# Spectral filter and gated feed-forward on one core: a later hold for the filter loads, and other PSUM banks and filler for the first batch's blocks

## The chip, the cores and the metric

One core of one Trainium2 chip. The metric is the device time of one execution in microseconds (us). Two things are used: the ratio of runs made on the same chip in the same rounds, and stage boundaries read from traces.

## The reference

```python
X = np.fft.rfft(x, axis=1)                      # x: (8, 3008, 256) float32
y = np.fft.irfft(X * (filt_r + 1j * filt_i)[None], n=3008, axis=1)
y = y.reshape(8 * 3008, 256)
out = (np.maximum(y @ w_gate, 0) * (y @ w_val)) @ w_out     # 256 -> 1536 -> 256
```

The kernel computes the transforms as matmuls in two steps (3008 = 94 x 32). A forward step over 94 (`psA`) goes out to device memory (`Abuf`) and comes back in another order (`at`). A forward step over 32 (`psX`), the products with the two filters (`tt`, `uu`) and an inverse step (`psD`) follow, then a second trip through memory (`Dbuf`, `dC`) and the last inverse step (`psY`). `psV`, `psG` and `psO` are the feed-forward part, which fills the rest of the time. Batches 1 to 7 are transformed in the shadow of the feed-forward blocks. Only batch 0 stands before the first of them, and only batch 0 is touched by this change.

## The kernel before

The parts that matter. Code of one engine runs in the order in which it is written here.

```python
def hold_gpsimd(tile_):                      # GpSimd waits until tile_ is there
    scr = sb.tile([128, 8], FP32, tag="scr", bufs=2)
    nc.gpsimd.tensor_copy(scr[:tile_.shape[0]], tile_)

def warm(n, cols=512):                       # filler: keeps TensorE's clock up
    psJ = ps.tile([128, 512], FP32, tag=fft_tag(True), name="psJ")
    for i in range(n):
        nc.tensor.matmul(psJ[:, :cols], junk[:, 0:128], junk[:, :cols], start=True, stop=True)
# ... the prologue:
load_x(0, nc.sync, ...)                      # x of batch 0 to XF[0], XF[1], 5 pieces
load_own_filters()
hold_gpsimd(XF[0][:, 2 * q - 8:2 * q])       # a quarter of x is there
for _ in filters:                            # the 7 other filter loads, on GpSimd's queue
    pass
warm(11)
for i, f in enumerate(items_a(0)):           # psA -> asb -> Abuf
    f()
    if i == 12:
        load_at(0, 0)
        load_at(0, 1)
for c in range(2, 4):
    load_at(0, c)
for half in range(2):
    for a in range(2):
        place_filter(0, a, half, nc.vector.tensor_copy)     # Ftr, waits for its loads
for i in range(3):
    make_back_t(i)                           # TensorE psI, VectorE copies it to I2t
warm(6)
place_filter(1, 0, 0, nc.vector.tensor_copy)
for i in range(3):
    make_back_u(i)                           # TensorE reads I2t
# ... place_own, the rest of Fti
for i in range(15):
    warm(2)                                  # 30 fillers until at is there
# ...
def first_b(amid):
    cuts = (0, 2, 4, 5, 6)
    for i in range(6):
        fwd(0, i)                            # psX, two banks by rotation over three pairs
        if i > 1:
            inv(0, i - 2, cuts=cuts)         # psD, the same rotation; ScalarE copies to dsb
        for e in range(2):
            product(0, i, e, 0)
            product(0, i, e, 1, pool=(i, e) in POOL_U)
        amid(i)                              # i < 2: warm(4, 256); else psA items of batch 1
    inv(0, 4, cuts=cuts)
    amid(6)
    inv(0, 5, cuts=cuts)
```

## Time and profile before

| | before |
|---|---|
| median of 4 runs (range) | 895.88 us (895.24 to 896.71) |
| span of the profiled run | 895.1 us |
| first forward block (`psX`) starts | 36.08 us |
| last `dsb` of first B ends | 53.32 us |
| first `psV` starts | 61.87 us |

Read it backwards. The feed-forward part is bound by TensorE and moves as a whole with its start, at 61.87. What counts is when the first `psX` starts, how long first B takes from there (53.32 - 36.08 = 17.24 us), and the last trip through memory.

### The profile page before, as it was taken

To read this page: it belongs to the slowest core of one execution; us is meant where nothing else is said; L and a number is where in the kernel's file an instruction comes from. 1 tells how busy PE (TensorE), PEld (TensorE's weight loads), DVE (VectorE), ACT (ScalarE), POOL (GpSimd) and SP (SyncE) were. 2 spreads that over 40 slices of the span, in tenths; PEclk is the share of its full clock that TensorE was granted. 3 is DMA by queue.
4 is the path that set the end of the run, shared out by engine and by line. 5 is a ranking of instruction groups with operands and counts; after the bars stand their busy time and mean duration, and the time that the engine had idled before them with its cause. 6 is when DMAs were issued, how large, how long until landed. Compare 5 with 4: busy or idle time off the path is not lost.

```text
span 895.1 us, 19152 instructions
## 1 busy us (share of the span) xinstructions
PE 878.4 (98%) x7206; PEld 507.2 (57%) x7206; DVE 569.2 (64%) x873; ACT 498.8 (56%) x891; POOL 364.4 (41%) x361
## 2 busy tenths in 40 slices
PE   7999999999999999999999999999999999999997
PEld 2335555556556665566655566555655566566665
DVE  2637766577665776666766676657776577655553
ACT  3475555555555556556555556555655555555552
POOL 4351698038661486416672167802867000000001
PEclk9999999999999999999999999999999999999999
DMA  8998448434466336463375334762445512331111
GB/s 229 281 242 170 131 132 179 110 102 121 122 152 135 117 95 146 129 139 94 97 175 139 92 99 108 179 139 78 118 138 148 121 31 80 81 74 36 37 34 51
DMA packets 114099, 109.18 MB, mean 122 GB/s; under 512 B 20359, under 2 KB 98599, under 8 KB 113366
## 3 DMA queue, kind: packets, MB, share of 16 engines
q1 hardware_dynamic: 90294, 80.10, 34.7%
q0 software_dynamic: 22992, 26.41, 12.3%
q8 instruction: 57, 0.93, 0.5%
q10 hardware_dynamic: 720, 1.45, 0.5%
q14 instruction: 36, 0.29, 0.1%
HBM read 61.93 MB, written 49.81 MB: 125 GB/s over the span
## 4 chain that ended last, share of the span: by engine, by line
PE 94%; DMA 2%; ACT 1%; POOL 1%; SPq 1%; DVE 1%; issue 1%; ACTq 0%; POOLq 0%
PE psV L467 28%; PE psG L467 27%; PE psO L486 27%; PE psF L323 3%; PE psD L394 2%; PE psY L451 2%; PE psX L364 2%; PE psA L276 1%; DMA XF<-in_x_dram 1%; PE psJ L520 1%; SPq L176 1%; DVE prod L472 0%; ACT dsb L401 0%; DMA dC<-Dbuf 0%; POOL out_dram L509 0%
## 5 line engine op out<-in xcount | busy, mean ns | idle before, releaser
L472 DVE SCALAR_TENSOR_TENSOR prod<-psG,vsb 128x512 bf16<-128x512 f32 x564 | 389.0, 690 | 263.4 <-ACT vsb L470 257.5
L470 ACT CAST vsb<-psV 128x512 bf16<-128x512 f32 x564 | 331.9, 589 | 263.2 <-PE psV L467 162.8
L467 PE MATMUL psV<-yT,WvT 128*128 128x512 bf16 x1128 | 336.6, 380 | 0.8 <-ACT asb L330 0.5
L486 PE MATMUL psO<-WoT,prod 128*128 128x256 bf16 x2256 | 336.5, 273 | 0.0
L467 PE MATMUL psG<-yT,WgT 128*128 128x512 bf16 x1128 | 335.5, 379 | 0.9 <-ACT dsb L401 0.3
L486 PEld LDWEIGHTS <-prod 128*128 128x128 bf16 x2256 | 220.3, 98 | 143.7
L467 PEld LDWEIGHTS <-WgT 128*128 128x128 bf16 x1128 | 109.9, 97 | 136.4 <-issue 3.4
L467 PEld LDWEIGHTS <-WvT 128*128 128x128 bf16 x1128 | 98.5, 98 | 41.8 <-issue 30.5
L258 POOL CAST scr<-prod 128x8 f32<-128x8 bf16 x24 | 4.5, 189 | 257.7 <-DVE prod L472 257.7
L509 POOL DMA_DIRECT2D out_dram<-osb x5 | 2.6, 536 | 195.9 <-ACT osb L499 195.9
L499 ACT COPY osb<-psO 128x512 f32<-128x512 f32 x92 | 53.9, 586 | 28.0 <-PE psO L486 26.6
L380 DVE TENSOR_TENSOR tt<-psX,Ftr 128x512 bf16<-128x512 f32 x96 | 65.1, 682 | 6.8 <-PE psX L364 6.8
L309 POOL TENSOR_TENSOR fold<-XP 128x1024 f32<-128x1024 f32 x24 | 56.6, 2357 | 20.8 <-PE psF L323 19.4
L380 DVE TENSOR_TENSOR uu<-psX,Fti 128x512 bf16<-128x512 f32 x89 | 60.5, 680 | 0.0
L401 ACT CAST dsb<-psD 128x512 bf16<-128x512 f32 x96 | 51.5, 589 | 12.5 <-PE psD L394 12.4
L296 POOL DMA_DIRECT2D XP<-in_x_dram x96 | 56.7, 596 | 3.2 <-PE psG L467 1.6
L310 POOL TENSOR_TENSOR XP<-XP 128x1024 f32<-128x1024 f32 x24 | 56.4, 2349 | 1.9
L330 ACT CAST asb<-psF 128x512 bf16<-128x512 f32 x48 | 25.8, 589 | 30.5 <-PE psF L323 30.5
L330 DVE CAST asb<-psF 128x512 bf16<-128x512 f32 x48 | 30.9, 686 | 18.6 <-PE psF L323 18.6
L456 ACT CAST yT<-psY 128x512 bf16<-128x512 f32 x47 | 27.5, 586 | 22.9 <-PE psY L451 22.6
L458 DVE CAST yT<-psY 128x512 bf16<-128x512 f32 x47 | 32.0, 681 | 9.7 <-PE psY L451 9.7
L451 PE MATMUL psY<-M,dC 96*128 96x94 bf16 (+18 forms) x604 | 37.5, 199 | 0.5 <-DMA dC<-Dbuf 0.4
(70 smaller groups left out, 493.3 us busy)
## 6 DMA issues: line engine op xcount, KB each, us to landing
at<-Abuf SPq DMA_DIRECT2D x32, 384.0 KB
dC<-Dbuf SPq DMA_DIRECT2D x64, 192.0 KB
XP<-in_x_dram POOLq DMA_DIRECT2D x48, 256.0 KB, 5.9
Dbuf<-dsb SPq DMA_DIRECT2D x23, 512.0 KB
XP<-in_x_dram POOLq DMA_DIRECT2D x96, 96.0 KB, 2.6
Abuf<-asb SPq DMA_DIRECT2D x96, 96.0 KB
out_dram<-osb SPq DMA_DIRECT2D x69, 94.0 KB
XF<-in_x_dram SPq DMA_DIRECT2D x15, 256.0 KB
```

Source lines behind the costliest of these rows:

```text
L296: nc.gpsimd.dma_start(xp[r:r + 24, 0:4:2, :], _ap(x, (b * N1 * N2 + o) * D, [[N2 * D, 24], [47 * N2 * D, 2], [1, 512]]))
L309: tt(t, xp[:, 0:2], xp[:, 2:4], op=ALU.add)
L310: tt(xp[:, 2:4], xp[:, 0:2], xp[:, 2:4], op=ALU.subtract)
L330: copy(asf[:, :, q, :], banks[q])
L380: nc.vector.tensor_tensor(p, psX, filt, op=ALU.mult)
L401: nc.scalar.copy(dsb[:, a, o:o + 2, :], psD[a])
L451: nc.tensor.matmul(psY[:, o:o + w], dCs[b, n2 // 8][:, n2 % 8, h * 128:(h + 1) * 128], M1[:, n1:n1 + w], start=True, stop=True)
L467: nc.tensor.matmul(pt[:, :W], w[:, h, ft * 128:(ft + 1) * 128], yt[:, h, :], start=(h == 0), stop=(h == 1))
L470: nc.scalar.copy(vsb, psV[:, :W])
L472: nc.vector.scalar_tensor_tensor(prod, in0=psG[:, :W], scalar=0.0, in1=vsb, op0=ALU.max, op1=ALU.mult)
L486: nc.tensor.matmul(psO[:, t % 2], prods[ft][:, t * 128:(t + 1) * 128], WoT[:, ft, :], start=(ft == 0), stop=(ft == NFT - 1))
L499: copy(osb[:, t0 % 2:t % 2 + 1], psO[:, t0 % 2:t % 2 + 1])
```

## The change

Its intent: x gets the DMA engines to itself for longer, so that the chain from x to `psX` ends sooner. Filler goes to where TensorE would otherwise idle in front of the first three forward blocks. Inverse blocks get banks of their own.

```diff
-    def fwd(b, i):
+    def fwd(b, i, junks=0):
         for e in range(2):
-            psXs[b, i, e] = ps.tile([128, 2, D], FP32, tag=fft_tag(), name="psX")
+            tag = "fft" if b or not e else "psv"
+            psXs[b, i, e] = ps.tile([128, 2, D], FP32, tag=tag, name="psX")
+            for _ in range(junks):
+                nc.tensor.matmul(psXs[b, i, e], junk[:, 0:128], junk, start=True, stop=True)
 ...
-        cuts = (0, 2, 4, 5, 6)
+        cuts, tags = (0, 2, 4, 5, 6), ("psg", "psg")
         for i in range(6):
-            fwd(0, i)
+            fwd(0, i, 2 if i < 3 else 0)
             if i > 1:
-                inv(0, i - 2, cuts=cuts)
+                inv(0, i - 2, tags, cuts)
 ...
-    hold_gpsimd(XF[0][:, 2 * q - 8:2 * q])
+    hold_gpsimd(XF[0][:, 4 * q - 8:4 * q])
 ...
     def amid(i):
-        if i < 2:
-            warm(4, 256)
-        else:
+        if i > 1:
             for _ in range((1, 1, 2, 1, 1)[i - 2]):
                 next(early)()
```

(The other lines of the diff move the tile `junk` up and pass `tags` on.)

## The prediction

> **What bounds the kernel now.** I read four views in this order: the page, the chain of work that ended last, the timeline engine by engine from 0 to 66 us, and the windows of one microsecond for the granted clock. First the page.
>
> ```profile
> PE 878.4 (98%) x7206; PEld 507.2 (57%) x7206; DVE 569.2 (64%) x873; ACT 498.8 (56%) x891; POOL 364.4 (41%) x361
> PE 94%; DMA 2%; ACT 1%; POOL 1%; SPq 1%; DVE 1%; issue 1%; ACTq 0%; POOLq 0%
> ```
>
> TensorE is busy for 98% of the span, and is 94% of the chain. The change touches nothing after batch 0, so it cannot shorten that part; it can only start it sooner. The first gate matmul of the main loop (psV) starts at 61.87 us of 895.1. So all that is at stake lies in the first 62 us, 7% of the span. A 2% verdict would need 18 us out of those 62.
>
> In that stretch "busy" misleads, because filler (psJ) counts as busy. The chain there shows it, from the last of x to the first forward block:
>
> ```profile
> 13.49 8.74 DMA XF<-in_x_dram
> 22.48 3.65 PE psA L276 x8
> 26.13 0.67 PE psI L192 x45
> 26.80 1.40 PE psJ L520 x6
> 28.20 0.74 PE psI L202 x3
> 28.94 6.49 PE psJ L520 x30
> 35.43 0.65 issue
> 36.08 0.46 PE psX L364 x8
> ```
>
> The columns are start, length and what. After the last piece of x come 3.65 us of forward DFT, then 9.30 us of set-up and filler in program order (0.67 + 1.40 + 0.74 + 6.49), then a 0.65 us gap until the first forward block at 36.08. What lands there is the fourth piece of at, as GpSimd's hold shows. Two holds on VectorE's side matter also:
>
> ```profile
> 17.85 0.95 DVE L238 COPY Ftr<-Ftr 32x3072 bf16<-32x3072 bf16 x1 [11.52 <-DMA Ftr<-in_filt_r_dram]
> 23.11 2.90 DVE L238 COPY Ftr<-Ftr 32x3072 bf16<-32x3072 bf16 x3 [4.30 <-DMA Ftr<-in_filt_r_dram]
> 26.43 2.08 DVE L197 CAST I2t<-psI 128x256 bf16<-128x256 f32 x6 [0.42 <-PE psI L192]
> 36.11 0.18 POOL L258 CAST scr<-at 32x8 f32<-32x8 bf16 x1 [22.30 <-DMA at<-Abuf]
> ```
>
> The filter copies wait for the filters at 23.11 and stand, in program order, ahead of the I2t copies that TensorE's last set-up step needs. The slack is 0.42 us. That is the tightest thing in the prologue.
>
> From 36 to 53 us (first B) the rows of ScalarE and TensorE say this:
>
> ```profile
> 39.11 5.63 POOL L378 TENSOR_TENSOR uu<-xs,Fti 128x512 bf16<-128x512 f32 x5 [1.08 <-ACT xs L377]
> 40.31 0.30 PE L394 MATMUL psD<-uu,I2u 64*64 64x256 bf16 x3 [0.93 <-POOL uu L378]
> 40.83 1.07 ACT L401 CAST dsb<-psD 128x512 bf16<-128x512 f32 x2 [0.61 <-PE psD L394]
> 43.94 1.07 ACT L401 CAST dsb<-psD 128x512 bf16<-128x512 f32 x2 [0.59 <-PE psD L394]
> 49.03 1.07 ACT L401 CAST dsb<-psD 128x512 bf16<-128x512 f32 x2 [0.20 <-PE psD L394]
> 52.25 1.07 ACT L401 CAST dsb<-psD 128x512 bf16<-128x512 f32 x2
> ```
>
> The first inverse block waits for GpSimd's first product at 40.3. From 40.83 to 53.32 ScalarE is hardly idle: 12 evictions of psD, 4 copies xs and 6 evictions asb. Only 0.59 and 0.20 us are marked as waits for psD. So ScalarE is close to the bound of this stage.
>
> Windows of the granted clock (the ninth number; window bounds first):
>
> ```profile
> 40.00:41.00 1.00, 0.69 (x12) 0.49 (x12) 0.80 (x2) 0.39 (x2) 1.00 (x2) 1.00 0.86 212
> 42.00:43.00 1.00, 1.00 (x13) 0.43 (x16) 0.00 (x0) 1.00 (x3) 1.00 (x2) 0.50 0.96 345
> 45.00:46.00 1.00, 1.00 (x23) 0.55 (x24) 0.32 (x1) 0.95 (x3) 0.27 (x1) 1.00 1.09 411
> ```
>
> TensorE waits at 38.7 to 40.3, and from about 41.1 to 44.6 it has half its clock.
>
> **What the Trainium skill says.** "TensorE: Matmul & The Clock Gate", Part 1 (The HAM clock gate): the clock is halved after an idle window of about 3.4 us, and given back after a busy one; the window runs freely. The trace agrees: about 3.5 us at 0.50, and the psA pair takes 1.65 us in it, against 0.86 outside. "DMA: Bandwidth & Descriptors", Queues, rings and completion order: each DMA engine takes turns between queues that have work. The trace agrees roughly: x (the SyncE queue) slows down once the filters (GpSimd's queue) run. "PSUM — Partial Sum Buffer", Terms: two engines must not touch one bank together, reads included. The program keeps to that: ScalarE's first xs waits until 38.44 for VectorE's tt of the same bank.
>
> **The change, part by part.** Times after the change are estimates from the rows above.
>
> (1) The hold. GpSimd waited for the second quarter of x, at 9.52; now for the whole first half, which TensorE met at 13.07. Seven filter transfers, issued from 10.01 to 13.8, move some 3.4 us later, to 13.4 to 17.2. The third piece of x took 3.58 us (psA starts at 9.49 and 13.07) with few filters about; the last two took 9.41 together (13.07 to 22.48), against 7.16 at that pace. So at most 2.25 us is to be had, and the filters are only away for the first third of it: I take 0.9. x is then all in at 21.6, psA ends at 25.2 instead of 26.13, and the last part of Abuf is written sooner by as much. But the DMA share was 1.1 all the way from 13 to 28.5, so bytes are moved in another order, not removed: at should land some 0.5 us sooner, near 35.5.
>
> (2) The filters' landing. Ftr came at 23.11, its last piece 12 us after its issue. It crawled while x ran, and ran fast after. Issued 3.4 us later, but with x gone 0.9 us sooner, I estimate 23.7 (23.0 to 24.7). Then VectorE is free at 23.7 + 2.90 = 26.6, I2t is copied by 28.7 instead of 28.51, and the 30 fillers end near 35.6 instead of 35.43. The 0.9 us that x gains is thus stopped at VectorE.
>
> (3) The filler ahead of fwd(0). It is four matmuls of 512 columns at 6.49/30 = 0.216 us, 0.87 us, ahead of the first forward block, where the four of 256 columns stood behind it. It runs while at is on its way: 35.6 + 0.87 = 36.5. So the first forward block starts at the later of 35.5 (at) and 36.5 (program order), against 36.08: +0.4 us.
>
> (4) Fillers ahead of fwd(1) and fwd(2), 0.87 us each, less 0.61 each removed. Behind fwd(0), VectorE needs 3 products (1.9 us) before it wants fwd(1), and fwd(1) is done after 1.75. No cost. fwd(2) now shares banks with fwd(0), so its second filler waits for xs(0,1), read at +2.96, and fwd(2) ends at +3.9 instead of +2.2. VectorE starts two products 0.45 us later, but then it had 2.29 us to wait anyway. The first inverse block still waits for GpSimd's product at +4.2. No cost, no gain.
>
> (5) The clock. TensorE's long idle stretch before 40.3 is cut to about 0.8 us, plus shorter waits. If the clock holds, the two cold psA pairs (1.65 and 1.30 against 0.86), fwd(3) and inv(1) give back about 0.79 + 0.44 + 0.23 + 0.45 = 1.9 us of TensorE. ScalarE has only 0.8 us of idle to give, so the stage shrinks by 0.8 at most, and 0.5 is my figure; I give the clock two chances in three.
>
> (6) The banks. Inverse blocks in their own pair no longer wait for the products of a later forward block, but each waits for the eviction of the one before. ScalarE always has an asb or xs between two evictions, which covers it: about zero.
>
> Sum: +0.4 (3) - 0.35 (5, weighed) - 0.2 for the Dbuf and dC transfers, which meet a little less traffic: about -0.2 us. So 896.0.
>
> **The rivals.** A: the filters become the wait. Ftr lands at 24.7 or later, VectorE's copies hold the I2t copies, and the first forward block slips to 37.5: +1.5 us, 897.5. For it: the slack of 0.42 us. Against it: the filters run two to three times faster once x is in. B: x's gain comes through. Ftr lands by 23.0, at by 35, the warm-up ends at 34.5, and with the clock held the gain is 0.7 + 0.8 = 1.5 us: 894.7. For it: the third piece's pace. Against it: a DMA share of 1.1. C: the single inverse pair serialises evictions with matmuls on ScalarE's path, some 0.3 us for each of six blocks, +1.8 us: 898.0. Against it: the work between them. D: all of it disappears into the wait for dC at 59.6; nothing changes, 896.2.
>
> **Range and chances.** All rivals lie within 2 us, and the main loop follows rigidly. The runs before spread over 1.2 us. I say 896.0, from 894.3 to 897.6. Faster than 2% would need 18 us: 0.01; slower 0.01; within 2% 0.98.
>
> **What would show it right or wrong.** The last psA block should start near 21.6 (step 1); VectorE's three Ftr copies at 23 to 24.7 (2); the first psX of at near 36.5, released by filler, not by DMA (3); the clock 1.00 throughout 40 to 46 and the psA pairs at 0.86 (5); the last dsb 16.8 us after the first forward block, against 17.2 (5, 6); psV 61 to 62. It is wrong if the first forward block comes before 35.3 or after 37.5, or if main-loop time after psV changes by over 0.5 us.

## More of the kernel before

Columns are start, length, queue, line, what.

```profile
24.21 1.85 SPq L350 DMA_DIRECT2D at<-Abuf  x2
26.77 0.31 SPq L282 DMA_DIRECT2D Abuf<-asb  x1
27.59 5.47 SPq L350 DMA_DIRECT2D at<-Abuf  x2
```

Two loads of `at`, the last write of `Abuf`, two more loads.

## The result, and the profile after

The changed kernel: median 896.15 us of 4 runs (894.01 to 897.11), against 895.88 before. The ratio is 0.9999, 95% interval 0.9978 to 1.0020: the same. (Ratios are the mean time of one kernel's runs over that of the other's of the same rounds, so not quite the ratio of the medians.) A second series on another chip, told below, gave 0.9992 (0.9979 to 1.0006).

The time stands still, but the first 62 us have changed in three places. First TensorE's timeline from the last half of x to the first forward block; the number in brackets is the idle time before the row and what ended it.

```profile
13.20 10.51 PE L277 MATMUL psA<-XF,WA 128*96 128x512 f32 x24 [1.94 <-DMA XF<-in_x_dram]
23.64 0.74 PE L193 MATMUL psI<-tabs,F 64*64 64x64 bf16 x48
27.54 0.39 PE L203 MATMUL psI<-I2t,tabs 128*128 128x512 bf16 x1 [1.76 <-DVE I2t L198]
29.23 8.02 PE L522 MATMUL psJ<-junk 128*128 128x512 bf16 x30
37.09 1.03 PE L363 MATMUL psX<-junk 128*128 128x512 bf16 x4
38.05 0.41 PE L368 MATMUL psX<-at,F 64*64 64x256 bf16 x8
```

After 13.20, `psA` runs without one wait and is done when `psI` starts at 23.64; before, `psI` started at 26.05. That is x's gain, 2.4 us. Then TensorE waits 1.76 us for I2t, which VectorE's timeline explains:

```profile
23.80 2.90 DVE L239 COPY Ftr<-Ftr 32x3072 bf16<-32x3072 bf16 x3 [1.55 <-DMA Ftr<-in_filt_r_dram]
26.73 2.08 DVE L198 CAST I2t<-psI 128x256 bf16<-128x256 f32 x6
```

The Ftr copies still wait for their loads until 23.80 (before: 23.11), and the I2t copies stand behind them. The wait then costs a second time. The 30 fillers end 8.02 us after their start, against 6.64 before, because TensorE's clock has fallen. In the windows of one microsecond the third number from the right is the granted clock:

```profile
28.00:29.00 1.00, 0.52 (x2) 0.20 (x2) 0.97 (x4) 0.94 (x2) 0.00 (x0) 0.80 1.01 263
30.00:31.00 1.00, 1.00 (x4) 0.36 (x3) 0.62 (x3) 0.07 (x1) 0.00 (x0) 0.50 1.06 345
32.00:33.00 1.00, 1.00 (x7) 0.40 (x5) 0.99 (x2) 0.00 (x0) 0.00 (x0) 0.99 0.26 82
42.00:43.00 1.00, 0.91 (x17) 0.49 (x12) 0.98 (x2) 0.39 (x2) 1.00 (x2) 1.00 1.17 401
```

The low clock of 41.1 to 44.5 before is gone: in first B the clock is now 1.00. But another low stretch stands at 28 to 32, in the filler. Four fillers ahead of the first block end the chain, at 38.05 instead of 36.08. `at` was not the bound: GpSimd's hold saw it land at 36.69.

From there first B goes faster. It ends at 54.50, so it lasts 16.45 us instead of 17.24. The marks on ScalarE's waits answer to those in the prediction:

```profile
50.00 1.07 ACT L405 CAST dsb<-psD 128x512 bf16<-128x512 f32 x2 [0.17 <-PE psD L398]
53.43 1.07 ACT L405 CAST dsb<-psD 128x512 bf16<-128x512 f32 x2
```

The waits of 0.59 and 0.20 us are down to one of 0.17 after the first inverse block. So in this trace the start comes 1.97 later, first B gives 0.79 back, and the transfers after it take 0.22 more. The first `psV` is at 63.27, 1.40 us late. The span is only 0.2 us longer, since the last write landed 1.0 us faster at the very end (5.00 us from the start of the last copy to the end of the span before, 3.98 after). Nothing in the change bears on that write. The trace of before is the odd one here: in the other eleven traces this tail lies between 3.8 and 4.4 us. That the two spans agree so closely is luck.

One thing more stands in SyncE's queue:

```profile
21.31 5.13 SPq L351 DMA_DIRECT2D at<-Abuf  x2
26.54 0.59 SPq L283 DMA_DIRECT2D Abuf<-asb  x1
27.23 6.37 SPq L351 DMA_DIRECT2D at<-Abuf  x2
```

`psA` ended 2.4 us sooner, and still the last write of `Abuf` leaves at 26.54, only 0.23 us sooner than before. ScalarE had filled its source by 24.32 (before: by 26.74, and the write left at once). Two loads of `at` stand ahead of it; the second waits for an earlier write of `Abuf` to land, and SyncE waits with it. In its list of waits, loads of `at` waited 8.9 us for writes of `Abuf`, 5.1 of them at once. The Trainium skill says in "DMA: Bandwidth & Descriptors", section Anatomy of one DMA (it describes GpSimd's path), that a semaphore wait "happens on the issuing sequencer before dispatch". SyncE's queue agrees in this trace: a write behind a waiting load was held up by it, here for 2.2 us (24.32 to 26.54).

So there are three questions. Is it VectorE's order that stops x's gain, and does the filler ahead of the first block cost its 0.87 us? Did clock or banks shorten first B? And is SyncE's order the next obstacle?

### The profile page after: what moved, and what is told of

Read it like the earlier page. It is cut to its first block, busy times and chain, and to the rows that moved or that the text cites. A ratio compares the mean times of both kernels' runs of the same rounds, so it can differ in the third digit from the quotient of the medians. Undisturbed runs are those within 1.5% of the kernel's fastest.

```text
span 895.3 us, 19036 instructions
## 1 busy us (share of the span) xinstructions
PE 873.4 (98%) x7089; PEld 508.4 (57%) x7210; DVE 568.9 (64%) x873; ACT 499.4 (56%) x891; POOL 364.7 (41%) x361
## 4 chain that ended last, share of the span: by engine, by line
PE 86%; DVE 4%; ACT 4%; DMA 3%; POOL 2%; issue 1%; SPq 0%; POOLq 0%; DVEq 0%; ACTq 0%
PE psG L471 26%; PE psO L490 25%; PE psV L471 24%; DVE prod L476 4%; ACT vsb L474 3%; PE psF L324 3%; PE psD L398 2%; PE psX L368 2%; PE psY L455 2%; DMA Fti<-in_filt_i_dram 1%; PE psJ L522 1%; PE psA L277 1%; POOL uu L382 1%; DMA XF<-in_x_dram 1%; DMA dC<-Dbuf 0%
## 5 line engine op out<-in xcount | busy, mean ns | idle before, releaser
L471 PE MATMUL psG<-yT,WgT 128*128 128x512 bf16 x1107 | 330.7, 379 | 6.9 <-DVE prod L476 0.8
L471 PE MATMUL psV<-yT,WvT 128*128 128x512 bf16 x1030 | 315.2, 380 | 0.8 <-ACT asb L331 0.5
L455 PE MATMUL psY<-M,dC 96*128 96x94 bf16 (+18 forms) x604 | 37.5, 198 | 0.7 <-DMA dC<-Dbuf 0.6
```

The lines of the kernel that those rows point to most:

```text
L455: nc.tensor.matmul(psY[:, o:o + w], dCs[b, n2 // 8][:, n2 % 8, h * 128:(h + 1) * 128], M1[:, n1:n1 + w], start=True, stop=True)
L471: nc.tensor.matmul(pt[:, :W], w[:, h, ft * 128:(ft + 1) * 128], yt[:, h, :], start=(h == 0), stop=(h == 1))
```

## The experiments

My theory: the hold works, but its gain meets VectorE's Ftr copies, and the wait that results lowers the clock in the filler; first B gains from the clock. The rivals: the filler at the head is the loss; `at`'s landing binds anyhow, because the DMA engines are full; the banks made first B shorter. Ten kernels were run, all gave correct results. The table has the stage boundaries of one trace of each, in us. "Gap" is TensorE's wait for I2t just before the I2u matmuls, "fillers" how long and how many, "`at`" the moment when GpSimd's hold saw it land.

| kernel | `psI` starts | gap | fillers | `at` | first `psX` | first B | first `psV` | ratio to before (95%) |
|---|---|---|---|---|---|---|---|---|
| before | 26.05 | none | 6.64 x30 | 36.11 | 36.08 | 17.24 | 61.87 | 1 |
| changed | 23.64 | 1.76 | 8.02 x30 | 36.69 | 38.05 | 16.45 | 63.27 | 0.9999 (0.9978 to 1.0020) |
| e9, changed again | 22.97 | 1.17 | 8.32 x30 | 35.34 | 36.94 | 16.45 | 61.79 | 0.9992 (0.9979 to 1.0006) |
| e1, hold only | 22.77 | 2.45 | 8.32 x30 | 36.67 | 37.15 | 16.66 | 62.41 | 1.0010 (0.9989 to 1.0031) |
| e2, all but the hold | 25.26 | none | 6.64 x30 | 35.79 | 35.72 | 16.44 | 60.68 | 0.9984 (0.9962 to 1.0006) |
| e3, no head filler | 23.23 | 1.77 | 6.64 x30 | 35.87 | 35.85 | 16.45 | 60.76 | 0.9985 (0.9963 to 1.0008) |
| e4, I2t first | 22.63 | none | 9.23 x42 | 35.18 | 35.38 | 16.44 | 60.40 | 0.9979 (0.9959 to 0.9999) |
| e5, banks only | 25.29 | 0.14 | 6.64 x30 | 37.70 | 37.67 | 17.52 | 63.65 | 0.9995 (0.9981 to 1.0009) |
| e6, filler only | 26.59 | none | 6.64 x30 | 35.82 | 36.74 | 16.67 | 62.13 | 1.0000 (0.9987 to 1.0012) |
| e7, `at` after `Abuf` | 22.76 | none | 7.07 x32 | 34.35 | 34.23 | 16.44 | 59.35 | 0.9981 (0.9968 to 0.9993) |
| e8, `Abuf` on ScalarE | 22.05 | none | 7.07 x32 | 33.77 | 33.64 | 16.44 | 58.81 | 0.9972 (0.9959 to 0.9984) |
| e10, e8 with the old hold | 25.64 | none | 5.34 x24 | 36.03 | 35.91 | 16.89 | 61.36 | 0.9989 (0.9977 to 1.0002) |

`psI` and `at` move from trace to trace of one kernel: by 0.7 and 1.35 us between the changed kernel and e9. What one trace alone shows within that is not argued from. As groups the two holds do part: `psI` starts at 25.26 to 26.59 in the five traces with the old hold and at 22.05 to 23.64 in the seven with the later one.

**e1: the hold alone.**

```diff
 # before.py
-    hold_gpsimd(XF[0][:, 2 * q - 8:2 * q])
+    hold_gpsimd(XF[0][:, 4 * q - 8:4 * q])
```

> The kernel before with the later filter hold alone. Theory (VectorE's Ftr copies stop x's gain, TensorE then idles about 1.8 us and runs its 30 fillers at half clock): psA ends near 23.7 us, TensorE idles 1.5 to 1.8 us before the I2u matmuls, the 30 fillers take 7 to 8 us, the first forward block starts at 36.8 to 37.3 us (no filler ahead of it), first B still lasts 17.2 us, and the time is 0.7 to 1.2 us above the kernel before. Rival (the filler ahead of the first block is the loss): the first block starts at 36.1 or earlier and the time is that of before or below it.

Measured: `psA` 3.3 us sooner, a gap of 2.45 us, fillers 8.32 us, first block at 37.15, with no filler ahead of it. The median is 897.61 against 896.70 for before on that chip, but the interval of the ratio includes 1. So in this trace the hold by itself makes the start later, not sooner. The gap and the fillers came out longer than expected. That first B takes 17.2 failed: it took 16.66, as the clock did not fall there in this trace.

**e2: all but the hold.**

```diff
 # after.py
-    hold_gpsimd(XF[0][:, 4 * q - 8:4 * q])
+    hold_gpsimd(XF[0][:, 2 * q - 8:2 * q])
```

> The changed kernel with the old filter hold. Theory: psA ends at 26.1 us and TensorE does not idle, the 30 fillers take 6.5 us, the four fillers ahead of the first block 0.87 us, so it starts at 36.3 us (before: 36.1); first B lasts 16.4 to 16.6 us instead of 17.2, clock 1.00 throughout; the time 0.4 to 0.7 us below the kernel before. Rival (the shorter first B came from the earlier transfers that the hold brings): first B stays at 17.2 us and the time is 0.2 us above before.

Measured: no gap, fillers 6.64, first B 16.44. The shorter first B does not come from the hold. The first block started at 35.72, released by `at`, rather than at 36.3 by the filler, since x came 0.8 us sooner than in the trace of before, with the same hold. Median 895.53 against 896.70; the interval just includes 1.

**e3: no filler ahead of the first block.**

```diff
 # after.py
-            fwd(0, i, 2 if i < 3 else 0)
+            fwd(0, i, 2 if 0 < i < 3 else 0)
```

> The changed kernel without the four fillers ahead of the first forward block; those ahead of the second and third stay. Theory: the first block starts when the 30 fillers end or when at has landed (36.7 us), whichever is later: 36.7 to 37.3 instead of 38.05, and the time is 0.8 to 1.3 us below the changed kernel. Rival (at's landing binds, and the filler is hidden): the first block starts at 38.0 again.

Measured: a first block at 35.85, held by `at`. Two things came together, and the trace parts them. The gap is there (1.77 us), yet the clock stayed at 1.00 in this run and the fillers took 6.64 us. The 2.20 us between this first block and that of the changed kernel's first trace come about so: the 30 fillers began 0.56 sooner (28.67 against 29.23) and ran 1.38 shorter (8.02 less 6.64), the head filler's 0.80 on the path fell away, and 0.54 of this was lost again in the wait for `at`. The first block came earlier than both theory and rival had it, as `at` landed earlier in this trace. The head filler is fully on the path where the fillers end after `at` lands (the changed kernel, e9), and hidden where they end before (e2).

**e4: I2t ahead of Ftr on VectorE.**

```diff
 # after.py
+    for i in range(3):
+        make_back_t(i)
     for half in range(2):
         for a in range(2):
             place_filter(0, a, half, nc.vector.tensor_copy)
-    for i in range(3):
-        make_back_t(i)
 ...
-    for i in range(15):
+    for i in range(21):
         warm(2)
```

> The changed kernel with VectorE's I2t copies ahead of its Ftr copies, and 42 warm-up fillers in place of 30, as they can now start sooner. Theory: TensorE does not wait for Ftr any more, the I2u matmuls run by 26.5 us, the fillers run at full clock and end at about 35.7, the first block starts at 36.6 to 36.9 us, bound by at's landing, first B lasts 16.5, and the time is 1.0 to 1.5 us below the changed kernel. Rival (the clock falls for another reason, or at lands later when the Ftr copies are later): the first block at 37.5 or later and no gain.

TensorE's timeline:

```profile
24.61 0.91 PE L203 MATMUL psI<-I2t,tabs 128*128 128x512 bf16 x3
25.36 9.23 PE L522 MATMUL psJ<-junk 128*128 128x512 bf16 x42
35.38 0.41 PE L368 MATMUL psX<-at,F 64*64 64x256 bf16 x8
```

The I2u matmuls follow at once, at 24.61 instead of 27.54, and 42 fillers run at full clock. VectorE's four Ftr copies now run from 25.12 to 28.99 and delay nothing: VectorE is free at 33.8, as before. The first block starts at 35.38. So VectorE's order is what made TensorE's set-up wait. It was not the last obstacle: e3, with the old order but a clock that held, got nearly as far (first `psV` at 60.76 against 60.40), as `at` landed at 35.87 and 35.18. The first block came 1.2 us before the range expected. The time is 0.21% below before, the interval just excludes 1.

**e5 and e6: the banks alone, the new filler alone.**

```diff
 # e5, after.py with the old hold
-            fwd(0, i, 2 if i < 3 else 0)
+            fwd(0, i)
 ...
-        if i > 1:
+        if i < 2:
+            warm(4, 256)
+        else:
 # e6, after.py with the old hold
-            tag = "fft" if b or not e else "psv"
+            tag = fft_tag()
 ...
-        cuts, tags = (0, 2, 4, 5, 6), ("psg", "psg")
+        cuts, tags = (0, 2, 4, 5, 6), None
 ...
-        psD = [ps.tile([128, 2, D], FP32, tag=tags[a], name="psD")
+        psD = [ps.tile([128, 2, D], FP32, tag=tags[a] if tags else fft_tag(), name="psD")
```

> Old hold, new bank pairs, old filler (four of 256 columns behind the first two forward blocks). What shortened first B from 17.24 to 16.45 us? If the clock alone (my theory: the stage took 16.66 in a run of the old banks in which the clock happened to hold): the idle stretch of TensorE before the first inverse block is back, the clock may fall to 0.50 within 40 to 45 us, and then the stage takes 17.0 to 17.3; should the clock hold by luck it takes 16.4. If the banks do it: 16.4 to 16.5 even with a clock that has fallen.

> Old hold, old banks, new fillers ahead of the first three forward blocks. Theory (the clock does it, the banks some 0.2 us): clock 1.00 throughout first B, stage 16.6 to 16.7 us. Rival (the banks do it): stage 17.0 or more at full clock.

Windows of e5 and then of e6, clock third from the right:

```profile
39.00:40.00 1.00, 1.00 (x8) 0.44 (x4) 1.00 (x3) 0.00 (x0) 0.63 (x1) 0.50 0.95 336
43.00:44.00 1.00, 1.00 (x2) 0.08 (x1) 0.00 (x0) 1.00 (x3) 1.00 (x1) 0.50 1.20 436
```

```profile
43.00:44.00 1.00, 0.39 (x14) 0.35 (x13) 1.00 (x2) 1.00 (x3) 1.00 (x2) 1.00 1.10 402
```

In e5 the clock is low from 38.6 to 45.4, twice as long as before (`at` came late in that run, and TensorE had already waited 1.94 us for it), and first B takes 17.52 us. So the banks alone do not hold it at 16.4 once the clock has fallen. Whether they help at a low clock stays open, as the low stretch was not the same length as before. In e6 the clock holds and the stage takes 16.67 with the old banks, as in e1. So 0.57 of the 0.79 us are the clock's (17.24 to 16.67), and the remaining 0.22 (16.67 to 16.45) go to the banks, at full clock. At full clock the figures repeat closely: 16.66 and 16.67 with the old banks, 16.44 or 16.45 in all seven traces with the new ones where VectorE was ready in time. Neither e5 nor e6 moved the whole time measurably.

**e7 and e8: SyncE's order.** Both are e4 with 32 fillers and one edit more.

```diff
 # e7
-        if i == 12:
-            load_at(0, 0)
-            load_at(0, 1)
-    for c in range(2, 4):
+    for c in range(4):
         load_at(0, c)
 # e8
-                eng = nc.scalar if b and c > 1 else nc.sync
+                eng = nc.scalar if c > 2 - b else nc.sync
```

> The kernel with I2t ahead of Ftr (e4), with all four pieces of at requested after the last write of Abuf in SyncE's order, and 32 fillers. Theory: in e4 the last write of Abuf is ready at 23.3 us, leaves at 24.2 behind two loads of at that wait in SyncE's queue, and lands only at 31.4, behind their transfers. Now it leaves at 23.4 and lands by 28; at is complete at 33.0 to 34.0 instead of 35.2, the first block starts at 33.5 to 34.2, and the time is 1.0 to 1.7 us below e4. Rival (DMA engines are saturated until 31.7 whatever the order): at is complete at 35 again, no gain.

> e4 with the last write of Abuf issued from ScalarE,[...] and 32 fillers. Theory: it leaves at 23.4 us and lands by 28, at is complete at 33.0 to 34.0, time 1.0 to 1.7 us below e4. Rival: saturated DMA engines, at complete at 35, no gain.

Of e8, ScalarE's queue, SyncE's queue, TensorE and GpSimd:

```profile
22.77 0.35 ACTq L283 DMA_DIRECT2D Abuf<-asb  x1
20.33 9.43 SPq L351 DMA_DIRECT2D at<-Abuf  x4
33.64 0.41 PE L368 MATMUL psX<-at,F 64*64 64x256 bf16 x8 [0.93 <-issue]
33.77 0.18 POOL L259 CAST scr<-at 32x8 f32<-32x8 bf16 x1 [17.84 <-DMA at<-Abuf]
```

The last write leaves right behind ScalarE's last eviction, the last load of `at` is issued by 29.8 us instead of 32.0 in e4, and `at` is there at 33.77 instead of 35.18. Of these 1.41 us, 0.58 lie before SyncE: `psA` ended that much sooner in this trace. The rival, that full DMA engines leave nothing to be had, falls, and not by these two times alone. The second number from the right in a window is the mean busy share of the DMA engines (it can exceed 1). First e4, then e8:

```profile
31.00:32.00 1.00, 1.00 (x6) 0.46 (x5) 0.99 (x2) 0.00 (x0) 0.00 (x0) 1.00 0.13 39
32.00:33.00 1.00, 1.00 (x6) 0.48 (x5) 0.99 (x2) 0.00 (x0) 0.00 (x0) 1.00 0.08 26
```

```profile
31.00:32.00 1.00, 1.00 (x6) 0.49 (x5) 0.99 (x2) 0.00 (x0) 0.00 (x0) 1.00 1.10 310
32.00:33.00 1.00, 0.71 (x4) 0.10 (x2) 0.97 (x3) 0.00 (x0) 0.00 (x0) 1.00 1.35 390
```

In e4 the engines stand nearly empty just before the last load of `at` gets under way. Such a hole (a share of 0.14 or less within 32 to 34 us) is in every trace but those of e7 and e8, in that of before too. e7 gets part of the gain: `at` at 34.35 and the first block at 34.23, both just later than expected.

The expected gain of 1.0 to 1.7 us over e4 shows in the first `psV` (1.05 and 1.59 us sooner), but not firmly in the time: e4 ran on another chip, and the ratios to before there and here (0.9979, then 0.9981 and 0.9972) lie within each other's intervals. e8 is the best version: median 893.34 us against 896.05 for before on the same chip, ratio 0.9972 (0.9959 to 0.9984). That is 0.3%, clear of noise. The changed kernel, in its own two series, stood at 0.9999 and 0.9992 to before. The intervals overlap a little and the two never ran on one chip, so that e8 is faster than the changed kernel is likely, but not shown by these times.

**e9: the changed kernel once more.** No edit.

> The changed kernel once more, unedited, for its spread and a second trace. Theory (TensorE waits some 1.8 us for I2t in every run, but whether the clock then falls depends on where the wait lies in the clock's window): psA ends at 22.8 to 23.8 us, the wait is there again, the 30 fillers take either 6.5 us (first block at 36.5 to 37.0) or 7.8 to 8.2 us (first block at 37.8 to 38.3); first B 16.45. The median lies within 0.7 us of the kernel before. Rival (the first trace was an odd one): no wait for I2t at all.

Measured: the gap is there (1.17 us, shorter than expected), the clock fell again and the fillers took 8.32 us. The median is 0.79 us below before, just outside the 0.7 expected. Ftr landed 1.3 us sooner than in the first trace, and so the first block started at 36.94. Of four traces with the later hold and Ftr ahead of I2t, three lost the clock in the filler (both of the changed kernel and e1), one did not (e3). None of the traces without such a gap lost it there. That chance of position in the clock's window (the freely running one that the prediction took from the Trainium skill) decides between these is the natural reading, but no run here sets that position, so it stays an inference.

**e10: the best version with the old hold.**

```diff
 # e8
-    hold_gpsimd(XF[0][:, 4 * q - 8:4 * q])
+    hold_gpsimd(XF[0][:, 2 * q - 8:2 * q])
 ...
-    for i in range(16):
+    for i in range(12):
         warm(2)
```

> The best version so far (I2t ahead of Ftr, last write of Abuf issued by ScalarE) with the old filter hold, and 24 fillers as its chain starts later. Is the hold worth anything once its gain is let through? Theory (yes: x then ends some 2.5 to 3.5 us later): psA ends at 25.3 to 26.2 us, at is complete at 35.0 to 36.0, the first block starts at 35.0 to 36.0 instead of 33.64, time 1.2 to 2.2 us above the best version. Rival (DMA bytes bound it whatever the order): at complete within 0.5 us of 33.8, no loss.

Measured: `psI` at 25.64 instead of 22.05, first block at 35.91 instead of 33.64, and first B 0.45 us longer, because VectorE, whose I2t copies wait for the later `psI`, is free only at 36.8. The first `psV` is 2.55 us later than in e8. The ratio to before is 0.9989 against 0.9972 for e8. The two were run on different chips, each against before there, and their intervals overlap. So in the traces the hold is worth about 2.5 of the 3.6 us that `psI` gains, once VectorE and SyncE let it through; the times point the same way without proving it.

## Why the prediction was right, point by point

The time was predicted as 896.0 and measured as 896.15; same was right. With 18 us needed for any other verdict, that was nearly certain. That the figure itself came so close is luck: terms that were off had opposite signs, and in the first trace a last write that landed 1.0 us faster hid a first `psV` 1.40 us late. The base was off too: 896.2 is 0.3 above the recorded median of 895.88, and the runs before spread over 1.47 us, not 1.2. (Rival A's own sum gives 897.7, not 897.5.)

- **The place and the size of what can be had.** Right: from the first `psV` to the start of the last copy of the output the loop took 828.23 us before and 828.05 after. Over all twelve traces it took 828.0 to 829.9, so a gain of a microsecond at `psV` need not show in one run's time. (The most was in e1, 829.94; I have not found out why.) My own sign of error, a main loop changed by over 0.5 us after `psV`, did appear if the tail is counted (833.2 to 832.0), by way of the last write described above.
- **Step 1, the hold.** The mechanism was right, the size not: 0.9 us for `psA`'s end, measured 2.4 and 3.1. I let the filters slow x for two thirds of its last half; in the trace `psA` never waited after 13.20. SyncE's queue moved 0.00 MB between 18 and 20 us, so x was all in by 18, and from then on TensorE's own pace (10.51 us for the row of `psA`) set the end. For `at` I predicted 35.5, on the grounds that the DMA engines are full. It landed at 36.69 and 35.34, against 36.11. The grounds were wrong: I had read the DMA share only up to 28.5, and in the trace of before it falls to 0.14 and 0.08 in the two microseconds from 32 to 34. What held `at` was the wait for the last write of `Abuf`, and in the changed kernel SyncE's order added to it, as e7 and e8 show.
- **Step 2, the filters.** The number was right: Ftr was predicted for 23.7 and landed at 23.80 (22.54 in e9), I2t for 28.7 and was copied by 28.81. The reason was not, so this is luck. In the trace of before GpSimd's queue, which carries the filters, did not run faster once x was in: it moved 0.73 MB in 14 to 22 us and 0.48 in 22 to 28, 0.09 and 0.08 MB per us. In the changed kernel it ran faster (0.87 MB in 18 to 24, 0.15 per us), as x was out of its way from 18 on. That TensorE's share of x's gain is stopped at VectorE is shown by e4.
- **Step 3, the first forward block.** Predicted 36.5, measured 38.05 and 36.94. The term that failed is "the 30 fillers end near 35.6": they ended at 37.25 and 36.14. Since x gained more than I thought, TensorE stood idle for 1.76 us before I2t came, and I did not ask what that does to the clock. It cost 1.4 us in the first trace and 1.7 in the second. By my own test (after 37.5 it is wrong) the first trace failed this step and the second passed. The filler at the head cost about what was said: 0.80 us on the path (37.25 to 38.05, and 36.14 to 36.94).
- **Step 4.** Right: the second filler of the third block waited for `xs`, the block ended 3.9 us after the first began, and VectorE then waited 0.45 us, at no cost to the end.
- **Step 5, the clock.** Right in kind: 1.00 throughout 36 to 48, and the `psA` pairs short again. But the trace of before had agreed with the skill's page only in the length of the slow stretch: TensorE's marked waits ahead of it were 0.35 and 0.93 us, far from an idle window of 3.4, and I passed over that. First B gained 0.79 us, the upper bound (0.8) rather than the weighed 0.35; of it the clock gave 0.57.
- **Step 6, the banks.** About right: 0.22 us where I had zero. Rival C, evictions made serial by one pair, did not occur.
- **The transfers after first B** were to give 0.2 us and gave none: from the last `dsb` to `psV` 8.55 us before, 8.77 and 8.40 after.

Rival A (VectorE's Ftr copies become the wait) was half right without Ftr being late: the order was enough. So the traces show where the gain went. x's 2.4 us turned into a wait for VectorE, then partly into a slow clock, and what was left would have met SyncE's order. Why the clock fell in three of four such traces stays open.

## What to carry to other kernels

When a transfer is made to land sooner, follow its consumers through every in-order queue on the way: here the gain was stopped first by copies for another operand on VectorE, and behind those by two waiting loads ahead of a ready store on SyncE. Put work whose input is ready ahead of work that waits, or on a queue of its own, before moving bandwidth about. And a new idle stretch on TensorE ahead of filler can have two prices, the wait and a slower clock after it (three of four such traces here), so compute the clock again wherever a wait moves.

## What the Trainium skill lacked or had wrong

- "TensorE: Matmul & The Clock Gate", Part 1, gives the re-throttle as following an idle window of about 3.4 us; further on it also tells of a kernel in which frequent short idles did it, without their length. Here the clock fell to 0.50 after much less than 3.4 us of idling: single gaps of 1.17 us (e9) and 1.76 us (changed kernel), each followed by three matmuls of 0.38 to 0.59 us with gaps of 0.3 us between them. The same pattern with a gap of 1.77 us in e3 did not lower it. How much load within a window suffices is not on the page. The low stretch itself fits the page's 3.4 us: worked out from the one-microsecond windows it lasted 3.4 us before, in the changed kernel, in e1 and in e9, and 6.8 in e5.
- The same page has no word on what filler should look like next to a wait. With four 512-column matmuls ahead of each of three blocks the clock stayed at 1.00 in all eight traces of first B that had them, and with two such blocks in e3; with four of 256 columns behind each of two it did so in one (e1) of three (before, e1, e5; in e5 a wait for `at` came first).
- "DMA: Bandwidth & Descriptors", Anatomy of one DMA, says that waits happen on the issuing sequencer. No page says what that can cost a store behind a waiting load. Here `at` landed 1.4 us sooner in e8 than in e4 (33.77 against 35.18), some 0.8 of it after `psA`'s earlier end is taken off, with the issuing engine of one write changed (and ten fillers fewer).
